# Eleven weight loads issued by ScalarE and not by GpSimd, and running products of 527 columns, in a fused attention, spectral and gating kernel

## The chip, the cores and the metric

The kernel runs on one core of a Trainium2 chip. Its five instruction streams are named as in the profile: PE is TensorE, DVE is VectorE, ACT is ScalarE, POOL is GpSimd and SP is SyncE. SPq, ACTq and POOLq are the instructions by which an engine starts a DMA transfer. The metric is the device time of one execution in microseconds (us); 0.2% of it, about 1.2 us, is what a measurement of this kernel can tell from no change.

## The reference

Three blocks follow each other on tensors of batch 4, sequence 768, width 384 (8 heads of 48). The second and the third get weights as 64-bit floats; the first has none.

```python
# block 1, per head: a decaying state
for t in range(S):
    state = alpha[:, :, t, :, None] * state + np.einsum('bhd,bhe->bhde', k[:, :, t], v[:, :, t])
    y[:, :, t] = np.einsum('bhd,bhde->bhe', q[:, :, t], state)
# block 2
theta = x @ w_theta
y = np.einsum('ts,bsd->btd', w_tok_r, x * np.cos(theta)) + np.einsum('ts,bsd->btd', w_tok_i, x * np.sin(theta))
u = x + y
x = u + np.maximum(u @ w_ch, 0.0)
# block 3
h = np.maximum(x @ w_in, 0.0); u, v = h[..., :512], h[..., 512:]
v_n = (v - v.mean(-1)) / np.sqrt(v.var(-1) + 1e-6)
out = (u * (np.einsum('ts,bsd->btd', w_spatial, v_n) + b_spatial)) @ w_out
```

## The kernel before

Block 1 is cut into 24 units `u` (4 batches, 6 stretches of 128 positions, each with two chunks of 64). A unit loads its decay factors (`load_al`, tile `al`), its queries and keys (`load_qk`) and its values (`load_v`). `att_scan` makes running products of the decay factors: on a line of 8 segments (one for each head of a partition's group) of `SEG` = 67 columns, so 536 in all, it scans backwards (L357), takes one reciprocal for each segment (L360) and scans forwards (L361). `att_qk` (L369) multiplies queries and keys by the result, and small matmuls (`att_a`, `att_k`, `att_u`, `att_y`) make the unit's output, which a pair of DMAs (`move_a`, L401, tile `ay`) feeds with half of its masked scores. Then come a transpose, the theta matmuls (`th_p`), sine and cosine on ACT, and the token mixing (`tokmix`, L610) that gathers a batch in PSUM.

The weights of block 2 come as 64-bit numbers and are made into pairs of 32-bit ones by pieces. A piece `n` passes through five steps. `raw_f64` (L233) starts the load of up to 772 KB into one of two `raw` buffers. `top` (ACT, L239) takes the top 16 bits, `join` (DVE, L248) joins them with the rest, `high` (ACT, L259) rounds and `low` (DVE, L267) takes the remainder; `low` needs `high`. Pieces 0 and 1 are the theta weights, 2 to 13 the token weights, 14 and 15 the channel weights; later ones belong to block 3. The first sixteen are started in the order 13, 1, 2, 0, 3, 7, 4, 8, 5, 15, 6, 9, 14, 10, 11, 12. Since there are two buffers, each load but the first two waits until `join` of the piece two places ahead has read its buffer: piece 2 waits for `join` of 13, piece 14 for `join` of 6.

GpSimd starts these sixteen (`c["queue"] = nc.gpsimd if n < NQ else nc.sync`, NQ = 16) and has little else to do until the third block. SP starts all other loads, save two at the very start that ACT starts. The order of all steps is a hand-kept list of numbers, `ORDER`; each engine runs its steps in that order, and waits for others by semaphores.

Of the kernel before, what the change touches and what calls it, by code (L numbers as in the profile page):

```python
# [35 lines left out]
SEG = 67  # L36
# [30 lines left out]
WM = 1  # L67
NQ = 16
# [64 lines left out]
def attention_mixer_kernel(  # L133
# [45 lines left out]

    p2 = ctx.enter_context(tc.tile_pool(name="p2", bufs=2))  # L180
    wst = ctx.enter_context(tc.tile_pool(name="wst", bufs=2))
# [821 lines left out]
    def load_cst():  # L1003
        nc.scalar.dma_start(cst_sb, cst)
# [435 lines left out]
```

## Time and profile before

| what | value |
|---|---|
| median of 3 runs | 584.64 us (584.15 to 585.07) |
| profiled execution, its own time | 583.91 us |
| its span, first to last instruction | 582.1 us |
| PE busy | 560.0 us (96%) |
| DVE busy | 440.7 us (76%) |
| ACT busy | 252.3 us (43%) |
| POOL busy | 25.1 us (4%) |
| chain that ended last | PE 78%, DVE 10% |

An engine's busy time is an average over stages. What the table does not tell is which engine sets the pace in which stage; that is read from the stretches and from the chain of waits.

### The profile page before, as it was taken

How to read it: one execution, taken by the hardware profiler on the slowest of the kernel's cores; microseconds unless marked ns; L12 is line 12 of the kernel's file. 1: busy time of each engine (PE TensorE's matmuls, PEld its weight loads, DVE VectorE, ACT ScalarE, POOL GpSimd, SP SyncE). 2: the span in 40 equal slices, each digit the busy share in tenths (PEclk: the TensorE clock that was granted, in tenths of full speed). 3: DMA queues.
4: the chain of work that ended last, by engine and by line, in shares of the span. 5: the costliest groups of instructions: out<-in, count | busy, mean ns of one | idle time of the engine just before them, and what ended most of it. 6: DMA issues, size and time to landing. Idle time of an engine off the chain costs nothing.

```text
span 582.1 us, 13446 instructions
## 1 busy us (share of the span) xinstructions
PE 560.0 (96%) x5737; PEld 508.6 (87%) x5737; DVE 440.7 (76%) x769; ACT 252.3 (43%) x474; POOL 25.1 (4%) x45
## 2 busy tenths in 40 slices
PE   2799999999999999999999999999999999999997
PEld 1667878888988889988989899999999899989997
DVE  7999999988788876878755887776665775677470
ACT  3476765535335533334554443534323441343222
POOL 1101100000000000000000100000000100011000
PEclk9999999999999999999999999999999999999999
DMA  7978746454253333333344525001002010211002
GB/s 266 327 240 273 268 158 214 120 191 130 84 171 107 104 91 127 122 106 96 95 133 173 182 81 192 1 0 57 25 2 96 28 42 0 82 42 41 1 1 81
DMA packets 28219, 66.23 MB, mean 114 GB/s; under 512 B 3072, under 2 KB 14336, under 8 KB 27904
## 3 DMA queue, kind: packets, MB, share of 16 engines
q1 hardware_dynamic: 25696, 53.14, 27.4%
q0 software_dynamic: 2176, 11.86, 5.9%
q8 instruction: 45, 0.74, 0.5%
q10 hardware_dynamic: 288, 0.37, 0.2%
q14 instruction: 14, 0.11, 0.1%
HBM read 52.78 MB, written 9.44 MB: 107 GB/s over the span
## 4 chain that ended last, share of the span: by engine, by line
PE 78%; DVE 10%; ACT 1%; DMA 1%; issue 1%; POOL 1%; POOLq 0%; DVEq 0%; ACTq 0%
PE acc L610 22%; PE acc L929 11%; PE pu L861 8%; PE psc L652 7%; PE po L987 6%; PE psv L788 6%; PE sp L900 4%; PE th L534 3%; PE psuy L466 3%; PE th L537 2%; PE psa L383 2%; PE psuy L424 2%; DMA raw<-in_w 1%; PE psk L407 1%; PE pst L494 1%
## 5 line engine op out<-in xcount | busy, mean ns | idle before, releaser
L610 PE MATMUL acc<-w,zs 128*128 128x256 f32 (+1 forms) x828 | 165.9, 344 | 0.0
L610 PEld LDWEIGHTS acc<-w,zs 128*128 128x128 f32 x828 | 128.2, 188 | 15.7
L788 PE MATMUL psv<-w,xs 128*128 128x512 f32 x216 | 53.6, 395 | 0.0
L861 PE MATMUL pu<-xs,w 128*128 128x384 f32 x288 | 53.1, 337 | 0.0
L987 PE MATMUL po<-w,gs 128*128 128x384 f32 x288 | 52.3, 336 | 0.3 <-ACT v L799 0.3
L987 PEld LDWEIGHTS po<-w,gs 128*128 128x128 f32 x288 | 50.2, 188 | 1.6 <-ACT v L799 0.7
L861 PEld LDWEIGHTS pu<-xs,w 128*128 128x128 f32 x288 | 50.4, 188 | 0.7 <-ACT o L997 0.3
L788 PEld LDWEIGHTS psv<-w,xs 128*128 128x128 f32 x216 | 40.0, 187 | 8.2 <-ACT v L799 0.2
L652 PE MATMUL psc<-us,wch 128*128 128x384 f32 (+1 forms) x243 | 41.2, 320 | 0.0
L652 PEld LDWEIGHTS psc<-us,wch 128*128 128x128 f32 x243 | 37.8, 189 | 0.8
L541 ACT ACTIVATE kk<-th,magic 128x384 f32<-128x384 f32 x24 | 13.9, 578 | 53.4 <-PE th L537 53.4
L973 ACT CAST gs<-t 128x384 fp32r<-128x384 f32 x32 | 15.8, 513 | 48.1 <-DVE t L966 48.1
L811 POOL TENSOR_TENSOR rs<-rs,mhalf 128x1 f32<-128x1 f32 x24 | 15.6, 652 | 441.6 <-DVE rs L808 441.6
L357 DVE TENSOR_TENSOR_SCAN al<-al,heads 112x536 f32<-112x536 f32 x24 | 30.5, 1269 | 3.2 <-DMA al<-in_al 3.2
L534 PE MATMUL th<-wth,xh 128*128 128x384 f32 x144 | 31.1, 352 | 1.2 <-DVE r L551 1.0
L361 DVE TENSOR_TENSOR_SCAN al<-al,heads 112x536 f32<-112x536 f32 x24 | 30.6, 1275 | 0.8
L929 PE MATMUL acc<-w,mx 128*128 128x384 f32 x162 | 30.7, 338 | 0.0
L929 PE MATMUL acc<-wt,vns 128*128 128x384 f32 x162 | 30.5, 337 | 0.0
L369 DVE TENSOR_TENSOR qk<-qk,al 112x1024 f32<-112x1024 f32 x24 | 29.3, 1219 | 0.1
L929 PEld LDWEIGHTS acc<-wt,vns 128*128 128x128 f32 x162 | 28.5, 188 | 0.1
L929 PEld LDWEIGHTS acc<-w,mx 128*128 128x128 f32 x162 | 28.5, 188 | 0.1
L239 ACT ACTIVATE zeros<-raw 128x768 f16<-128x768 bf16 (+1 forms) x22 | 22.9, 1043 | 11.6 <-DMA raw<-in_w 11.6
(122 smaller groups left out, 975.7 us busy)
## 6 DMA issues: line engine op xcount, KB each, us to landing
qk<-in_qk SPq DMA_DIRECT2D x24, 512.0 KB, 4.7
raw<-in_w POOLq DMA_DIRECT2D x14, 772.0 KB, 6.1
vd<-in_v SPq DMA_DIRECT2D x24, 288.0 KB, 3.7
al<-in_al SPq DMA_DIRECT2D x23, 268.0 KB, 3.5
raw<-in_w SPq DMA_DIRECT2D x6, 772.0 KB, 5.4
out<-o SPq DMA_DIRECT2D x24, 192.0 KB, 1.9
x2d<-xT SPq DMA_DIRECT2D x6, 576.0 KB, 4.6
ay<-ax SPq DMA_DIRECT2D x48, 64.0 KB, 2.8
```

Of the source, the lines that this page charges most:

```text
L239: nc.scalar.activation(out, c["top"].rearrange("p (c k) -> p c k", k=4)[:, :, 0], AF.Identity, scale=0.5)
L357: nc.vector.tensor_tensor_scan(out=back[:, ::-1], data0=line[:, ::-1], data1=one[:, ::-1], initial=1.0, op0=ALU.mult, op1=ALU.add)
L361: nc.vector.tensor_tensor_scan(out=line, data0=line, data1=one, initial=0.0, op0=ALU.mult, op1=ALU.add)
L369: nc.vector.tensor_tensor(out=x, in0=x, in1=st[u]["ar"], op=ALU.mult)
L534: nc.tensor.matmul(th, xh[:, 0, k], wth[:, pr, k], start=(k == 0 and pr == 0), stop=False)
L610: nc.tensor.matmul(acc[b, n][:, c0:c1], zs[:, pl, ri, m * 128:(m + 1) * 128], w[:, pr, t0:t1], start=first and n != 1, stop=last, skip_gro ...
L652: nc.tensor.matmul(ps, wch[:, pl, k, m * 128:(m + 1) * 128], us[:, pr, k], start=(n == 0), stop=(n == 3 * KD - 1),)
L788: nc.tensor.matmul(ps, xs2[:, pl, k, o:o + 128], win[pr, "v"][:, k], start=(n == 0), stop=(n == 3 * KD - 1),)
L861: nc.tensor.matmul(pu, win[f // 2][:, pl, k * 256 + f % 2 * 128:k * 256 + f % 2 * 128 + 128], xq[b, h][:, pr, k], start=(n == 0), stop=(n ...
L900: nc.tensor.matmul(sp[:, :TH], vns[b, s][:, pl, f * 128:(f + 1) * 128], wsp[s][:, pr, t], start=(n == 0), stop=(n == 3 * NS - 1),)
L929: nc.tensor.matmul(g, left(b, n, j, pl, c), right(n, j, pr), start=(n in (1, 5, 6) and i == 0), stop=(i == 3 * NJ - 1), skip_group_check=n ...
L987: nc.tensor.matmul(po, gs[b][:, pl, f, s * 128:(s + 1) * 128], wo[f // 2][:, pr, f % 2 * DM:(f % 2 + 1) * DM], start=(n == 0), stop=(n == ...
```

## The change

Three edits, of which the first two do something to the running kernel:

- Pieces 2, 0, 3, 7, 4, 8, 5, 15, 6, 9 and 14 (the third to the thirteenth in the order of loading) are started by ACT. Pieces 13, 1, 10, 11 and 12 stay with GpSimd.
- A segment has 66 columns in place of 67. The marks of `heads` move from a segment's first column to its last, the backward scan leaves out the line's first column and the forward scan its last, so each runs over 527 columns in place of 536; a load of decay factors has 264 KB in place of 268.
- The step `warm` gets the number 0 in place of the last number. All numbers in `ORDER` move up by one, and each engine's steps stand in the order in which they stood. New options that are off (ZA, GQ, RS, RP, AH, FIN, SA) come along.

```diff
-SEG = 67
+SEG = 66
+RA = (2, 0, 3, 7, 4, 8, 5, 15, 6, 9, 14)
...
-    nc.vector.memset(heads[:, :, 0:1], 1.0)
+    nc.vector.memset(heads[:, :, SEG - 1:SEG], 1.0)
...
-            c["queue"] = nc.gpsimd if n < NQ else nc.sync
-            k = step(0.0, "queue" if n < NQ else "dma", 2.4 * size, raw_f64, n, after=before, tiles=[raw])
+            c["queue"] = nc.scalar if n in RA else nc.sync if n in RS or n >= NQ else nc.gpsimd
+            k = step(0.0, "act" if n in RA else "dma" if n in RS or n >= NQ else "queue", 2.4 * size, raw_f64, n, after=before, tiles=[raw])
...
+    def scans(u, g0, g1, which):
+        al, rt, one = (x[:, g0:g1].rearrange("p g j -> p (g j)") for x in (st[u]["al"], st[u]["rt"], heads))
+        if "b" in which:
+            nc.vector.tensor_tensor_scan(
+                out=rt[:, :0:-1], data0=al[:, :0:-1], data1=one[:, :0:-1], initial=1.0, op0=ALU.mult, op1=ALU.add
+            )
+        if "i" in which:
...
+                nc.vector.reciprocal(out=out, in_=total)
+        if "f" in which:
+            n = (g1 - g0) * SEG - 1
+            nc.vector.tensor_tensor_scan(out=al[:, :n], data0=al[:, :n], data1=one[:, :n], initial=1.0, op0=ALU.mult, op1=ALU.add)
...
     def att_scan(u):
-        nc.vector.tensor_tensor_scan(
-            out=back[:, ::-1], data0=line[:, ::-1], data1=one[:, ::-1], initial=1.0, op0=ALU.mult, op1=ALU.add
-        )
-        nc.vector.reciprocal(out=al[:, :, 1:2], in_=rt[:, :, 2:3])
-        nc.vector.tensor_tensor_scan(out=line, data0=line, data1=one, initial=0.0, op0=ALU.mult, op1=ALU.add)
+            scans(u, 0, 8, "f" if u in RP else "bif")
...
-    step(0.0, "act", 0.3, warm)
```

On GpSimd, the loads of the kernel before stood in one row from the start of the program (`raw` is the buffer, `in_w64` cut to `in_w` the weights; the pieces of 1552 columns are the half-sized ones, 1 and 15):

```order
L218 MEMSET zeros 128x768
L233 DMA raw<-in_w 128x3088
L233 DMA raw<-in_w 128x1552
L233 DMA raw<-in_w 128x3088 x7
L233 DMA raw<-in_w 128x1552
L233 DMA raw<-in_w 128x3088 x6
L811 ISA
```

Now there are five: pieces 13 and 1 at the start, and 10, 11 and 12.

```order
L230 MEMSET zeros 128x768
L245 DMA raw<-in_w 128x3088
L245 DMA raw<-in_w 128x1552
L245 DMA raw<-in_w 128x3088 x3
L863 ISA
```

On ACT, the start of the program read as follows in the kernel before (L239 is `top`, L259 `high`, L411 copies keys, L482 and L506 copy a unit's output and its transpose, L501 rounds that):

```order
L239 ACTIVATE zeros<-raw 128x768
L411 COPY kt<-acc 128x448
L259 ACTIVATE w<-wf 128x768
L239 ACTIVATE zeros<-raw 128x384
L259 ACTIVATE wth<-wf 128x384
L239 ACTIVATE zeros<-raw 128x768
L411 COPY kt<-acc 128x448
L482 COPY x<-psy 128x4x48 x2
L239 ACTIVATE zeros<-raw 128x768
L506 COPY xT<-pst 128x3x128
L259 ACTIVATE wth<-wf 128x768
L501 CAST xh<-pst 128x384
```

Now the loads of pieces 2, 0, 3 and 7 stand among these, most of them right ahead of the `high` (L271) that waits for the same `join`. In brackets are the semaphores that a row waits for: DVE is the `join` whose buffer is reused, DMAHW the landing of an earlier transfer started by SP or ACT (eight semaphores are shared in turn by all of those).

```order
L454 COPY kt<-acc_125 128x448 [waits PE_49]
L245 DMA raw<-in_w 128x3088 [waits DVE_49]
L271 ACTIVATE w<-wf 128x768
L251 ACTIVATE zeros<-raw 128x384 [waits DMASW1_49]
L245 DMA raw<-in_w 128x3088 [waits DMAHW2_49,DVE_49]
L271 ACTIVATE wth<-wf 128x384
L251 ACTIVATE zeros<-raw 128x768 [waits DMAHW7_49]
L245 DMA raw<-in_w 128x3088 [waits DMAHW5_49,DVE_49]
L454 COPY kt<-acc_224 128x448 [waits PE_49]
L530 COPY x<-psy 128x4x48 [waits PE_49] x2
L251 ACTIVATE zeros<-raw 128x768 [waits DMAHW2_49]
L554 COPY xT<-pst 128x3x128 [waits PE_49]
```

Around the load of piece 14, the last that ACT starts, the rows of ACT were these before:

```order
L580 CAST zs<-z 128x768
L411 COPY kt<-psk 128x448
L259 ACTIVATE w<-wf 128x768
L541 ACTIVATE kk<-th,magic 128x384
L239 ACTIVATE zeros<-raw 128x768
```

Now the load stands between the copy of keys and `high` of piece 6, for whose `join` both wait:

```order
L628 CAST zs<-z 128x768
L454 COPY kt<-psk 128x448
L245 DMA raw<-in_w 128x3088
L271 ACTIVATE w<-wf 128x768
L589 ACTIVATE kk<-th,magic 128x384
L251 ACTIVATE zeros<-raw 128x768
```

## Rows read from the trace of the kernel before

**Rows 1.** Three stretches: bounds and length in us, busy us (instructions) by engine, clock, DMA

```profile
14.50:29.00 14.50, 10.28 (x191) 8.88 (x192) 13.22 (x22) 7.08 (x13) 2.05 (x4) 0.91 0.95 329
36.00:87.00 51.00, 49.51 (x702) 38.98 (x696) 50.08 (x77) 35.70 (x64) 4.65 (x9) 1.00 0.71 240
87.00:500.00 413.00, 412.53 (x4239) 378.27 (x4238) 313.94 (x551) 173.02 (x330) 11.60 (x18) 1.00 0.30 98
```

**Rows 2.** Two pieces of the chain that ended last: start us, us, what

```profile
60.27 7.96 DMA raw<-in_w
...
86.70 1.07 PE acc L610 x6
```

**Rows 3.** DVE in order of time: start us, us, instruction, idle time before it

```profile
10.54 0.93 DVE L248 SCALAR_TENSOR_TENSOR wf<-raw,zeros 128x768 uint32<-128x768 uint32 x1
...
12.38 0.96 DVE L267 SCALAR_TENSOR_TENSOR w<-wf,w 128x768 fp32r<-128x768 f32 x1
...
17.35 0.96 DVE L248 SCALAR_TENSOR_TENSOR wf<-raw,zeros 128x768 uint32<-128x768 uint32 x1 [0.73 <-ACT zeros L239]
...
24.80 0.55 DVE L519 TENSOR_TENSOR xh<-pst,xh 128x384 fp32r<-128x384 f32 x1
...
32.91 0.55 DVE L551 SCALAR_TENSOR_TENSOR r<-kk,th 128x384 f32<-128x384 f32 x1 [0.60 <-ACT kk L541]
...
45.65 0.95 DVE L267 SCALAR_TENSOR_TENSOR w<-wf,w 128x768 fp32r<-128x768 f32 x1
...
61.04 0.95 DVE L267 SCALAR_TENSOR_TENSOR w<-wf,w 128x768 fp32r<-128x768 f32 x1
...
69.38 0.96 DVE L248 SCALAR_TENSOR_TENSOR wf<-raw,zeros 128x768 uint32<-128x768 uint32 x1 [0.65 <-ACT zeros L239]
```

**Rows 4.** POOL starts the loads of pieces 2, 7 and 14

```profile
11.77 0.53 POOL L233 DMA_DIRECT2D raw<-in_w  x1 [9.12 <-DVE wf L248]
...
23.78 0.53 POOL L233 DMA_DIRECT2D raw<-in_w  x1 [4.65 <-DVE tmp L447]
...
60.27 0.53 POOL L233 DMA_DIRECT2D raw<-in_w  x1 [7.19 <-ACT kt L411]
```

**Rows 5.** ACT in order of time, around the same pieces

```profile
11.51 0.84 ACT L259 ACTIVATE w<-wf 128x768 fp32r<-128x768 f32 x1 [0.79 <-DVE wf L248]
...
16.25 1.07 ACT L239 ACTIVATE zeros<-raw 128x768 f16<-128x768 bf16 x1 [1.55 <-DMA raw<-in_w]
...
24.27 0.46 ACT L501 CAST xh<-pst 128x384 fp32r<-128x384 f32 x1
...
31.37 1.08 ACT L239 ACTIVATE zeros<-raw 128x768 f16<-128x768 bf16 x1 [2.46 <-DMA raw<-in_w]
...
44.63 0.84 ACT L259 ACTIVATE w<-wf 128x768 fp32r<-128x768 f32 x1 [0.94 <-DVE wf L248]
...
60.05 0.84 ACT L259 ACTIVATE w<-wf 128x768 fp32r<-128x768 f32 x1
...
68.26 1.09 ACT L239 ACTIVATE zeros<-raw 128x768 f16<-128x768 bf16 x1 [0.63 <-DMA raw<-in_w]
```

**Rows 6.** ACT starts a transfer at the program's start: start us, us

```profile
1.17 0.46 ACTq L342 DMA_DIRECT2D al<-in_al  x1
```

**Rows 7.** SP starts transfers: start us, us, instruction, count

```profile
39.45 1.11 SPq L401 DMA_DIRECT2D ay<-ax  x2
...
91.56 0.33 SPq L233 DMA_DIRECT2D raw<-in_w  x1
...
113.13 1.16 SPq L347 DMA_DIRECT2D qk<-in_qk  x1
```

**Rows 8.** DMA issues of whole pieces: KB each, median us from issue to landing

```profile
raw<-in_w POOLq DMA_DIRECT2D x14, 772.0 KB, 6.1
...
raw<-in_w SPq DMA_DIRECT2D x6, 772.0 KB, 5.4
```

**Rows 9.** DVE to 87 us, scan groups: busy us, mean ns of one | idle before

```profile
L361 DVE TENSOR_TENSOR_SCAN al<-al,heads 112x536 f32<-112x536 f32 x8 | 10.2, 1275 | 0.3
```

More of the change, by code (lines that the diff above doesn't have):

```diff
@@ L67 @@
 WM = 1
+ZA = 0
+AQ = (("load_cst",), ("load_al", 1))
+GQ = ()
+RA = (2, 0, 3, 7, 4, 8, 5, 15, 6, 9, 14)
+RS = ()
+RP = ()
+AH = 0
+FIN = 0
+SA = ()
 NQ = 16
@@ L334, in attention_mixer_kernel, with issuer @@
     tmps = {}
+    def issuer(*key):
+        return nc.scalar if key in AQ else nc.gpsimd if key in GQ else nc.sync
     def load_al(u):
@@ L346, in load_qk @@
         st[u]["qk"] = t[:112]
-        nc.sync.dma_start(t, qk_in[u])
+        issuer("load_qk", u).dma_start(t, qk_in[u])
     def load_v(u):
@@ L351, in load_v, with att_half, att_back, att_inv @@
         st[u]["vd"], st[u]["vn"] = v[:, 0:2], v[:, 2]
-        nc.sync.dma_start(v.rearrange("p c a e -> p (c a e)"), v_in[u])
-    def att_scan(u):
-        al, rt = st[u]["al"], st[u]["rt"]
-        line, back, one = (x.rearrange("p g j -> p (g j)") for x in (al, rt, heads))
-        nc.vector.tensor_tensor_scan(
-            out=back[:, ::-1], data0=line[:, ::-1], data1=one[:, ::-1], initial=1.0, op0=ALU.mult, op1=ALU.add
-        )
-        nc.vector.reciprocal(out=al[:, :, 1:2], in_=rt[:, :, 2:3])
-        nc.vector.tensor_tensor_scan(out=line, data0=line, data1=one, initial=0.0, op0=ALU.mult, op1=ALU.add)
+        issuer("load_v", u).dma_start(v.rearrange("p c a e -> p (c a e)"), v_in[u])
+    def scans(u, g0, g1, which):
[5 more added lines that the diff above has]
+        if "i" in which:
+            out, total = st[u]["al"][:, g0:g1, 0:1], st[u]["rt"][:, g0:g1, 1:2]
+            if u in RP:
+                nc.gpsimd.tensor_tensor(out=out, in0=total, in1=minus_one[:112, None, :].to_broadcast([112, g1 - g0, 1]), op=ALU.pow)
+            else:
+                nc.vector.reciprocal(out=out, in_=total)
+        if "f" in which:
+            n = (g1 - g0) * SEG - 1
+            nc.vector.tensor_tensor_scan(out=al[:, :n], data0=al[:, :n], data1=one[:, :n], initial=1.0, op0=ALU.mult, op1=ALU.add)
+    def att_half(u):
+        scans(u, 0, 4, "bif")
+    def att_back(u):
+        scans(u, 0, 8, "b")
+    def att_inv(u):
+        scans(u, 0, 8, "i")
+    def att_scan(u):
+        if AH and u == 0:
+            scans(u, 4, 8, "bif")
+        else:
+            scans(u, 0, 8, "f" if u in RP else "bif")
     def decay(u, c):
         rt = st[u]["rt"].rearrange("p (a c) j -> p a c j", c=2)
-        return rt[:, :, c, 2:3].to_broadcast([112, NP, D])
+        return rt[:, :, c, 1:2].to_broadcast([112, NP, D])
     def att_qk(u):
@@ L400, in move_a @@
         for par in range(2):
[L401 removed]
+            issuer("move_a", u).dma_start(ay[64 * par:64 * par + 64], ax[64 * (1 - par):64 * (1 - par) + 64])
     def att_k(u):
@@ L433, in att_s @@
         tmp = st[u]["psu", 0][:112] if c and summed(u) else tmps.pop(0)
+        if (u, c) in SA:
+            rt = st[u]["rt"].rearrange("p (a c) j -> p a c j", c=2)
+            for a in range(NP):
+                nc.scalar.activation(ss[:, a], tmp[:, a], AF.Identity, scale=rt[:, a, c, 1:2])
+            return
         nc.vector.tensor_tensor(out=ss, in0=tmp, in1=decay(u, c), op=ALU.mult)
@@ L997, in o_e, with o_l, o_x @@
         nc.scalar.copy(out=o, in_=s2.pop(("po", b, s)))
+    def o_l(b, s, n):
+        if n == 0:
+            s2["o", b, s] = s2["o"].rearrange("p (n e) -> p n e", n=2)[:, take("o", (b, s))]
+        c = slice(n * DM // 2, (n + 1) * DM // 2)
+        (nc.vector.tensor_copy if n else nc.scalar.copy)(out=s2["o", b, s][:, c], in_=s2["po", b, s][:, c])
+    def o_x(b, s, n):
+        c = slice(n * DM // 2, (n + 1) * DM // 2)
+        (nc.sync if n else nc.scalar).dma_start(out[b, s * 128:(s + 1) * 128, c], s2["o", b, s][:, c])
     def o_d(b, s):
@@ L1003, in load_cst @@
     def load_cst():
-        nc.scalar.dma_start(cst_sb, cst)
+        issuer("load_cst").dma_start(cst_sb, cst)
     def warm():
@@ L1012, in negate, with by @@
                 nc.scalar.activation(x, ident, AF.Identity, scale=-1.0)
-    step(0.0, "dma", 0.32, load_cst)
+    def by(*key):
+        return "act" if key in AQ else "queue" if key in GQ else "dma"
+    step(0.0, "act", 1.5, warm)
+    step(0.0, by("load_cst"), 0.32, load_cst)
     if XLP or THP:
@@ L1134, in attention_mixer_kernel @@
             continue
-        step(0.0, "dve", 0.41, acc_zero, b, tiles=[ta[1]])
+        step(0.0, *(("act", 0.5) if ZA else ("dve", 0.41)), acc_zero, b, after=[("load_cst",)] if ZA else [], tiles=[ta[1]])
     for b in range(B):
@@ L1356, in attention_mixer_kernel @@
             t += 2.09
+            if FIN and b == B - 1 and s == NS - 1:
+                e = [step(0.0, x, 0.25, o_l, b, s, n, after=[k], tiles=[ps, o, ("zeros", 1, "o")]) for n, x in enumerate(("act", "dve"))]
+                for n in range(2):
+                    step(0.0, "dma" if n else "act", 0.65, o_x, b, s, n, after=e[n:n + 1], tiles=[o, ("zeros", 1, "o")])
+                continue
             k = step(0.0, "act", 0.375, o_e, b, s, after=[k], tiles=[ps, o, ("zeros", 1, "o")], by=t + 1.0)
```

43 lines of the change are left out of this document (32 added, 11 removed), and 100 rows, old and new, of the table ORDER.

## The prediction

> **What bounds the kernel now.** I read the stretches first [rows 1]. From 87 to 500 us PE is busy 412.53 of 413.00 us: nothing that shortens another engine there moves the end, and whatever moves the point at which PE gets into this stretch moves the end one for one. Between 36 and 87 us it is DVE that has no time left (50.08 of 51.00 us), while PE has 1.5 us of gaps. The chain of waits says the same: it runs along DVE up to 86 us and along PE from 86.70 us [rows 2]. So the change, all of which lies ahead of 87 us save scans, is worth what it does to DVE's order of work there.
>
> DVE loses little to waits, and the reader should see whom it waits for [rows 3]: 0.73 us at 17.35 and 0.65 us at 69.38 for ACT's `top`, which itself waited for a piece to land [rows 5]; 0.60 us at 32.91 for ACT's L541, which stands right behind the `top` of piece 7, and that one had waited 2.46 us for its landing [rows 5]. These three, 1.98 us, hang on late pieces.
>
> **The change, part by part.**
>
> *Scans.* A scan takes 1275 ns for 536 columns [rows 9], 2.4 ns a column with its fixed part spread over all; 9 columns fewer are 9 x 2.4 = 21 ns. Eight units of two scans lie ahead of 87 us, so 16 x 21 = 0.34 us of DVE at most. Some of it, in the first 36 us, only lengthens a wait; I take 0.25 us. The scans behind 87 us lie beside PE's work and are worth nothing. The 1.5% smaller load of decay factors is nothing that a row here could show.
>
> *Loads leave GpSimd.* That frees 11 x 0.53 us of an engine that is idle [rows 4], worth nothing by itself. What counts is when a piece lands. `join` of piece 13 ends at 10.54 + 0.93 = 11.47 [rows 3]; ACT goes on 0.04 us later, at 11.51 [rows 5], GpSimd starts piece 2 only at 11.77 [rows 4]. An ACT that is free starts a load 0.26 us sooner. From issue to landing the medians are 6.1 us for pieces from GpSimd and 5.4 us for the later ones from SP [rows 8], under different loads of the DMA engines, which move 329 GB/s at a busy share of 0.95 between 14.5 and 29 us [rows 1]. With the DMA engines so full the bounds of the difference are 0 and 0.7 us, and a loss of 0.25 us isn't excluded either. I take 0.25 us of gain, nearer to the full stretch.
>
> *Loads enter ACT's row.* ACT started a transfer in 0.46 us [rows 6]; SP took 0.33 us for a single one of these pieces, 0.55 us for each of a pair, and 1.16 us once [rows 7]. I take 0.42 us, between the single piece and the pair, since some of these come just beside SP's. Eleven are 4.6 us of an engine that is busy 35.70 of 51 us [rows 1], and whoever stands behind one in ACT's row waits for it. Most stand right ahead of the `high` for whose `join` both wait, so no new wait for DVE arises, only the 0.42 us. Each load also waits for the landing of a transfer eight such transfers earlier. For piece 6, started after the `high` of 44.63, that is the first of SP's pair at 39.45, over 5 us before [rows 5, 7], and for the others the distance is larger; I put that at nothing.
>
> *Where it comes out on DVE.* I follow it from wait to wait.
>
> 1. Piece 2 goes ahead of `high` at 11.51. DVE's `low` started at 12.38, 0.03 us behind the end of that `high` (12.35) [rows 3, 5]: it slips by 0.42 us, less 0.08 us for four shorter scans, 0.34 us. At 17.35 DVE had 0.73 us to spare. Piece 2 starts 0.26 us sooner and lands 0.25 us sooner, so DVE needs to wait no longer than to 16.84, and it now arrives at 17.35 - 0.73 + 0.34 = 16.96. It is 0.4 us ahead.
> 2. The masked scores of unit 0 came in the delayed part, so their transfer and the unit's output come 0.34 us later, hence ACT's copy, `top` and `join` of piece 0; then piece 7 goes ahead of `high` of piece 0 and L501. DVE's L519 at 24.80 followed ACT's L501 (24.27 + 0.46 = 24.73) at once [rows 3, 5]: 0.34 + 0.42, less a scan or two, is 0.7 us behind.
> 3. At 32.91 DVE had 0.60 us to spare. Piece 7 starts at about 23.9 in place of 23.78 and lands 0.25 us sooner: ACT's `top` of 31.37 comes 0.1 us sooner, so does L541, and DVE with it. What was lost at 24.80 is gone, 0.1 to 0.2 us ahead.
> 4. From there to 69 us DVE has no gap to lose anything in. Where `low` had some slack behind `high`, that is taken off: piece 15's load delays a `high` that ended at 45.47 for a `low` at 45.65 (0.24 us exposed), piece 14's one that ended at 60.89 for a `low` at 61.04 (0.27 us) [rows 3, 5]. With the other loads, which stand behind a `high` or beside longer work, 0.5 us; DVE is then 0.3 us behind.
> 5. At 69.38 the wait of 0.65 us for piece 14 takes that up too. This is the last wait for a piece that ACT starts, so what counts at the end is when piece 14 lands. ACT can start it at 60.23, behind its copy of keys, so 0.04 us sooner than GpSimd at 60.27 [rows 4]; with 0.25 us of quicker landing that is 0.29 us. DVE arrives at 69.38 - 0.65 + 0.3 = 69.03, in time for the `join` at 69.09.
>
> *Sum.* 0.29 us ahead at 69.38, 0.08 us more from the four scans up to 87 us, and 0.1 us given back where PE and ACT need the delayed results: about 0.25 us, which PE carries to the end. The profiled execution would take 583.91 - 0.25 = 583.7 us; it lies 0.73 us below the median of 584.64 us, so as a median I forecast 584.4 us, no change that can be told from none.
>
> A rule speaks against the term of landing. The Trainium skill, DMA: Bandwidth & Descriptors, section "Issuing engines are not separate DMA queues", says that transfers run on the same 16 DMA engines whichever engine starts them, and that a change of issuer saves only sequencer time. By it the 0.25 us fall away and the sum would be 0.0 us.
>
> **The rivals.**
>
> *Faster.* ACT's issues are covered: they begin while ACT still works on what stands ahead of them, and cost what SP's single one cost or less. Then the 1.98 us of late pieces may vanish, with 0.34 us of scans: 2.3 us at most, 1.2 us when half of the waits and all scans go. PE's clock helps: it was granted at 0.91 of full speed from 14.5 to 29 us [rows 1], so some of this stretch ran at the lower of its two levels, 1.2 GHz; if PE is fed more steadily there, up to 0.09 x 14.5 = 1.3 us of it come back, of which DVE could use the 0.60 us at 32.91. Against it: `join` frees the buffer late and ACT waits for that same `join`, so in most places nothing covers the issue. I place it at 583.0 us.
>
> The same side has another mechanism: the descriptors of GpSimd's transfers are held up while DVE works, and ACT's would not be. The trace shows an even 0.53 us for each of the three issues [rows 4], also with DVE busy all the time, so nothing of a hold-up in the issue itself; piece 14 took 7.96 us to land all the same [rows 2]. By this mechanism it would land 1.5 to 2 us sooner, and by step 5 the gain ends where DVE arrives: 0.35 + 0.08 us, 584.2 us, still within the forecast's own range. The Trainium skill, DMA: Bandwidth & Descriptors, section "SWDGE vs HWDGE vs iDMA", states this rule: GpSimd writes descriptors into SBUF, from which DVE locks it out in some modes, and transfers started by ACT are immune.
>
> *Slower.* An issue on ACT, between running activations and beside SP's, takes as long as SP's longest, 0.8 to 1.16 us. Its place is step 4: with 1.0 us an issue the exposed parts are 0.82 us for piece 15, 0.85 us for piece 14 and, as an estimate, about half an issue each for pieces 6 and 9, which stand beside longer work, 2.6 us in all, and the 0.65 us at 69.38 can't take them up: 2.6 - 0.65 = 1.9 us and more, 586.5 to 587 us. It decides from about 0.7 us an issue. For it: ACT is the one engine besides DVE that is in every loop of this stretch. Against it: ACT's own row says 0.46 us.
>
> *It doesn't do what it says.* The order shows the loads on ACT, so this is left out.
>
> **How the numbers follow.** Forecast (within 0.2%, 1.2 us either way): 0.58. Faster by more: 0.26, the covered issue or the steadier clock. Slower by more: 0.16, the long issue. The likeliest time is 584.4 us. The forecast's own bounds: an issue of 0.33 us and 0.7 us of quicker landing give 0.9 us of gain; an issue of 0.6 us and a landing 0.25 us later give 1.1 us of loss: 583.7 to 585.7 us as a median. To reach half-way into both rivals I take 582.9 to 586.0 us.
>
> **What would show it.** In the profile after: ACTq issues of 0.33 to 0.6 us (0.7 us or more: slower); DVE's waits at 17.35 and 32.91 nearly gone, that at 69.38 at most halved, with small new ones behind ACT's `high` and its rounding of transposes (L501 here); the medians of landing from ACT about 0.25 us under those from GpSimd; scans of about 1.25 us; the chain still turning from DVE to PE near 86 us. I am wrong if PE gets into its unbroken stretch more than 1.2 us away from now, or if it no longer stays full afterwards.

## Result and profile after

The changed kernel is slower: 588.28 us median (587.17 to 591.68, 7 runs) against 584.64 us (583.91 to 585.23, 7 runs) for the kernel before; the ratio is 1.0077 with an interval of 1.0058 to 1.0096. Run again it had 587.63 us against 584.64 us, ratio 1.0051 (1.0037 to 1.0065). Forecast was no change, 584.4 us (582.9 to 586.0 us); the time lies outside the range.

The profiled execution took 587.17 us with a span of 585.1 us, 3.26 us more than that of the kernel before. I read it in the order of the prediction. First the three stretches (columns as in [rows 1]):

```profile
14.50:29.00 14.50, 11.04 (x193) 9.57 (x193) 13.12 (x23) 6.91 (x12) 0.00 (x0) 1.00 0.90 329
36.00:87.00 51.00, 48.53 (x710) 38.48 (x699) 49.65 (x77) 35.74 (x63) 1.58 (x3) 1.00 0.72 243
87.00:500.00 413.00, 412.50 (x4230) 377.44 (x4229) 312.40 (x548) 173.31 (x331) 11.61 (x18) 1.00 0.30 97
```

POOL has nothing left to do in the first stretch, and the clock is 1.00 there where it was 0.91 [rows 1]. In the last one PE is as full as before (412.50 of 413.00 us) and got through 4230 matmuls where it got through 4239. That count alone tells little, since it moves with what the ends of the stretch cut off: with 66 columns alone (e7 below), at the pace of before, it is 4230 too. Whether a full engine has become slower has to be read between two fixed moments.

The scans and the landings, as groups (columns as in [rows 8] and [rows 9]):

```profile
raw<-in_w ACTq DMA_DIRECT2D x10, 772.0 KB, 4.8
raw<-in_w SPq DMA_DIRECT2D x6, 772.0 KB, 4.9
raw<-in_w POOLq DMA_DIRECT2D x4, 772.0 KB, 7.1
```

```profile
L389 DVE TENSOR_TENSOR_SCAN al<-al,heads 112x527 f32<-112x527 f32 x8 | 10.0, 1256 | 0.3
L378 DVE TENSOR_TENSOR_SCAN al<-al,heads 112x527 f32<-112x527 f32 x8 | 10.0, 1250 | 3.0 <-DMA al<-in_al 3.0
```

A scan is 19 ns shorter, as forecast (21 ns). Pieces from ACT land in 4.8 us (6.1 us from GpSimd [rows 8]; the four that are left with it, the very first among them, take 7.1 us). But in front of the backward scan (L378) stand 3.0 us of waits for a load of decay factors (1.6 us before, all of it in the first 10 us); 0.8 us of them are in the stretch where DVE has no time left.

DVE in order of time (columns as in [rows 3]); L260, L279, L482 and L495 are L248, L267, L434 and L447 of before:

```profile
11.06 0.93 DVE L260 SCALAR_TENSOR_TENSOR wf<-raw,zeros 128x768 uint32<-128x768 uint32 x1
...
13.28 0.96 DVE L279 SCALAR_TENSOR_TENSOR w<-wf,w 128x768 fp32r<-128x768 f32 x1 [0.72 <-ACT w L271]
...
22.43 0.36 DVE L495 TENSOR_TENSOR tmp<-acc,ss 112x192 f32<-112x192 f32 x1 [1.03 <-PE acc L467]
...
25.98 0.56 DVE L567 TENSOR_TENSOR xh<-pst,xh 128x384 fp32r<-128x384 f32 x1 [0.28 <-ACT xh L549]
...
41.62 1.26 DVE L378 TENSOR_TENSOR_SCAN al<-al,heads 112x527 f32<-112x527 f32 x1 [0.80 <-DMA al<-in_al]
```

The waits at 17.35, 32.91 and 69.38 us [rows 3] are gone, where the forecast had left up to half of the last one. New are 0.72 us behind ACT's `high` at 13.28 us, 1.03 us for PE at 22.43 us and 0.80 us for the decay factors of unit 4.

ACT and its queue (columns as in [rows 5] and [rows 6]), the load of piece 2, the `high` of piece 13, `top` of piece 7, the loads of pieces 8 and 14:

```profile
12.03 0.34 ACTq L245 DMA_DIRECT2D raw<-in_w  x1
12.41 0.84 ACT L271 ACTIVATE w<-wf 128x768 fp32r<-128x768 f32 x1 [1.41 <-DVE wf L260]
...
31.45 1.08 ACT L251 ACTIVATE zeros<-raw 128x768 f16<-128x768 bf16 x1 [1.96 <-DMA raw<-in_w]
...
35.45 0.34 ACTq L245 DMA_DIRECT2D raw<-in_w  x1
...
60.89 0.33 ACTq L245 DMA_DIRECT2D raw<-in_w  x1
```

An issue costs 0.33 to 0.35 us. `high` begins 0.42 us behind the end of `join` (11.06 + 0.93), where it was 0.04 us.

### The profile page after: what moved, and what is told of

Its sections match the earlier page's. It is cut to its first block, busy times and chain, and to the rows that moved or that the text cites. A ratio compares the mean times of both kernels' runs of the same rounds, so it can differ in the third digit from the quotient of the medians.

```text
span 585.1 us, 13439 instructions
## 1 busy us (share of the span) xinstructions
PE 561.8 (96%) x5737; PEld 510.4 (87%) x5737; DVE 439.9 (75%) x769; ACT 252.7 (43%) x474; POOL 19.1 (3%) x34
## 4 chain that ended last, share of the span: by engine, by line
PE 79%; DVE 11%; DMA 4%; ACT 3%; issue 2%; POOL 1%; ACTq 0%; DVEq 0%; POOLq 0%; SPq 0%
PE acc L658 23%; PE acc L981 10%; PE pu L913 7%; PE psc L704 7%; PE po L1039 7%; PE psv L840 6%; PE sp L952 4%; PE th L582 4%; PE psuy L514 3%; DMA raw<-in_w 3%; PE th L585 2%; PE psa L426 2%; PE psuy L467 2%; DVE wf L260 1%; PE psk L450 1%
## 5 line engine op out<-in xcount | busy, mean ns | idle before, releaser
L378 DVE TENSOR_TENSOR_SCAN al<-al,heads 112x527 f32<-112x527 f32 x24 | 30.0, 1250 | 4.6 <-DMA al<-in_al 4.4
L389 DVE TENSOR_TENSOR_SCAN al<-al,heads 112x527 f32<-112x527 f32 x24 | 30.1, 1256 | 0.8
L582 PEld LDWEIGHTS th<-wth,xh 128*128 128x128 f32 x144 | 25.2, 193 | 3.8 <-ACT xh L549 2.5
```

The costliest lines, as they stand in the source:

```text
L378: nc.vector.tensor_tensor_scan(out=rt[:, :0:-1], data0=al[:, :0:-1], data1=one[:, :0:-1], initial=1.0, op0=ALU.mult, op1=ALU.add)
L389: nc.vector.tensor_tensor_scan(out=al[:, :n], data0=al[:, :n], data1=one[:, :n], initial=1.0, op0=ALU.mult, op1=ALU.add)
L582: nc.tensor.matmul(th, xh[:, 0, k], wth[:, pr, k], start=(k == 0 and pr == 0), stop=False)
```

## Where the 3.26 us are

To split the account I take two moments that every kernel has: the start of the last `psk` matmuls (L407 of before) ahead of PE's full stretch, and the start of ACT's last copy of an output. Between them nearly everything is PE, one matmul behind the other. In order of time (start us, us, instruction), of the kernel before:

```profile
86.09 0.51 PE L407 MATMUL psk<-cst_sb,qk 112*128 112x112 f32 x3 [0.54 <-DVE ax L391]
...
578.89 0.48 ACT L997 COPY o<-po 128x384 f32<-128x384 f32 x1 [1.60 <-PE po L987]
```

and of the changed kernel:

```profile
86.64 0.60 PE L450 MATMUL psk<-cst_sb,qk 112*128 112x112 f32 x4 [0.54 <-DVE ax L434]
...
581.51 0.48 ACT L1049 COPY o<-po 128x384 f32<-128x384 f32 x1 [1.63 <-PE po L1039]
```

So PE gets to its full stretch 0.55 us later, needs 494.87 us for it and not 492.80 us (2.07 us more), then come 3.55 us to the span's end (3.24 us before, 0.31 us more) and 2.11 us outside the span (1.78 us, 0.33 us more). 0.55 + 2.07 + 0.31 + 0.33 = 3.26 us. This is the account of one execution of each kernel; the medians are 3.64 us apart.

The largest part lies where the prediction had placed nothing of the change but a few scans of no worth. The diff holds one thing that the section on the change left out and the prediction did not price: a constant that no instruction uses.

```diff
     nc.vector.memset(mhalf, -0.5)
+    minus_one = const.tile([128, 1], F32, name="minus_one")
+    if RP:
+        nc.vector.memset(minus_one, -1.0)
```

RP is empty, so nothing is written; but by the program's layout the constant takes 32 bytes of each partition, and the tiles that are laid out behind it, the weights `w` among them, move up by 32 bytes. Tiles laid out from the other end (`zs`, `gs`) stay. The traces hold no addresses; where this document speaks of them, it goes by the layout.

## Experiments

Each kernel is compared with runs of the kernel before on the same chip. The last columns are from the profiled execution: start of `psk`, and the time from there to the last copy.

| kernel | median us | before us | ratio (interval) | psk us | to last copy us |
|---|---|---|---|---|---|
| before | | | | 86.09 | 492.80 |
| changed | 588.28 | 584.64 | 1.0077 (1.0058-1.0096) | 86.64 | 494.87 |
| e1 changed, again | 587.63 | 584.64 | 1.0051 (1.0037-1.0065) | 87.11 | 494.82 |
| e2 constant alone | 586.34 | 584.64 | 1.0029 (1.0017-1.0040) | 85.48 | 494.50 |
| e3 changed, no constant | 586.56 | 584.64 | 1.0037 (1.0017-1.0057) | 88.71 | 493.21 |
| e4 eleven loads alone | 586.50 | 584.64 | 1.0043 (1.0023-1.0063) | 86.96 | 493.18 |
| e5 without piece 8 | 586.32 | 584.39 | 1.0032 (1.0019-1.0045) | 87.92 | 493.41 |
| e6 piece 8 alone | 585.06 | 584.39 | 1.0013 (0.9998-1.0028) | 87.33 | 492.77 |
| e7 66 columns alone | 583.20 | 584.39 | 0.9980 (0.9968-0.9993) | 85.03 | 492.83 |
| e8 two constants | 585.39 | 584.39 | 1.0007 (0.9995-1.0020) | 87.03 | 493.56 |
| e9 piece 8 later | 586.67 | 584.58 | 1.0048 (1.0019-1.0077) | 88.34 | 493.17 |
| e10 eleven loads, again | 587.55 | 584.58 | 1.0051 (1.0028-1.0074) | 85.99 | 493.31 |
| e11 66 columns, piece 8 on SP | 584.10 | 584.58 | 0.9999 (0.9988-1.0011) | 85.56 | 492.83 |
| e12 constants on both sides | 585.31 | 584.58 | 1.0009 (1.0000-1.0019) | 86.02 | 493.52 |
| e13 first four loads | 585.16 | 584.31 | 1.0015 (1.0001-1.0029) | 88.84 | 493.15 |
| e14 last seven loads | 584.32 | 584.31 | 1.0005 (0.9991-1.0019) | 87.93 | 493.06 |
| e15 without piece 2 | 586.75 | 584.31 | 1.0035 (1.0021-1.0050) | 87.14 | 492.86 |
| e16 six loads behind `high` | 584.48 | 584.31 | 1.0009 (0.9995-1.0024) | 87.99 | 492.91 |
| e17 66 columns, again | 584.11 | 584.12 | 0.9996 (0.9984-1.0009) | 86.44 | 492.84 |
| e18 mended change | 584.94 | 584.12 | 1.0009 (0.9995-1.0024) | 88.60 | 492.84 |

The start of `psk` moves by up to 3.8 us between profiled executions, and by 1.0 and 1.4 us between two executions of one kernel (e4 and e10, e7 and e17), so of that column a single number proves little. The last column repeats within 0.05 us (changed and e1), 0.01 us (e7 and e17) and 0.13 us (e4 and e10).

### Taking the change apart (e1 to e4)

e1 is the changed kernel as it is.

> The changed kernel once more, on the chip of the next three. All theories: 1.005 to 1.010 of the kernel before, as in its first runs (1.0077). If the runs fall again into a group near 587.5 us and one near 591 us, and those near 591 us have a lower mean granted clock, the slower group is PE's clock; if they don't, the first spread was the chip's.

e2, on the kernel before:

```diff
     nc.vector.memset(mhalf, -0.5)
+    minus_one = const.tile([128, 1], F32, name="minus_one")
```

> The kernel before with nothing but one more constant of 4 bytes, never used, which the changed kernel also allocates; it moves the weights, the transposes and most later tiles by 32 bytes. Layout theory (PE's cadence in its full stretch drifts by 0.4% because its operands start at other addresses): +1.5 to +2.5 us, the drift between 87 and 560 us there again, the turn to PE still at 86.7 us. Loads theory (all of the loss comes from ACT's loads and the clock): no change, 584.6 us within 0.5 us.

e3 takes the three lines of the constant out of the changed kernel.

> The changed kernel without the unused constant, so the large tiles lie where they lay before. Layout theory: 1.5 to 2.5 us faster than the changed kernel, about 585.2 us, no drift behind 87 us. Loads theory: as the changed kernel, 587 to 588.5 us.

e4, on the kernel before:

```diff
+RA = (2, 0, 3, 7, 4, 8, 5, 15, 6, 9, 14)
-            c["queue"] = nc.gpsimd if n < NQ else nc.sync
+            c["queue"] = nc.scalar if n in RA else nc.gpsimd if n < NQ else nc.sync
```

> The kernel before with the eleven loads started by ACT alone; 67 columns a segment, no new constant. Layout theory: within 0.8 us of the kernel before (585 us), since only the 0.5 us at the turn to PE is left. Loads theory: +2.5 to +4 us, with or without a second group of runs at a lower clock.

The constant alone costs 0.29%, and its cost lies where theory had it: 494.50 us from `psk` to the last copy, 1.70 us more than before, with `psk` not later. Without it the changed kernel needs 493.21 us there and is still 0.37% slower. The loads alone cost 0.43%, 0.38 us of it between the two moments. 1.70 + 0.38 = 2.08 us, the 2.07 us of the changed kernel. The six executions of e1 lie between 586.91 and 588.05 us, with no group near 591 us; what the spread of the first runs up to 591.68 us was stays open.

### What the constant does (e8, e12)

e8 has a second unused constant, so that the tiles move by 64 bytes:

```diff
     nc.vector.memset(mhalf, -0.5)
+    minus_one = const.tile([128, 1], F32, name="minus_one")
+    minus_two = const.tile([128, 1], F32, name="minus_two")
```

> The kernel before with two unused constants of 4 bytes and not one, so that the weights and the other tiles behind the constants move by 64 bytes and not by 32: their addresses stand to multiples of 64 bytes as before. Theory (alignment to 64 bytes): PE's cadence in the stretch from 87 to 560 us is that of the kernel before (about 174 ns for L987), 584.6 us. Rival (any move, or the mere presence of a constant): 586.3 us, PE 1.5 us later over this stretch as with one constant. Rival (by the distance): 64 bytes cost twice as much, 588 us.

e12 has one on the left, and one at the far end of each pool on the right, so that the left tiles move up by 32 bytes and the right ones down by 32:

```diff
+    minus_one = const.tile([128, 1], F32, name="minus_one")
...
     def open_b():
+        pb.tile([128, 1], F32, name="pad_b")
         pb_stack.close()
...
             gs[b] = mpb[0].tile([128, 2, KF, S], F32R, tag="gs", name="gs", bufs=1)
+            if b == 0:
+                mpb[0].tile([128, 1], F32, name="pad_c")
```

> The kernel before with the unused constant of 4 bytes on the left side and one on the right side of the memory, so that nearly all tiles, those on the left 32 bytes up and those on the right 32 bytes down, stand at a multiple of 64 bytes (before: nearly all 32 bytes off such a multiple). Theory A (the two operands of a matmul want the same place within 64 bytes): PE's lines on w and zs, w and gs have their cadence of before (L610 191.6 ns, L987 173.8 ns start to start), 584.6 us. Theory B (where w itself stands counts): the drift of 1.5 us from 87 to 560 us is there as with the left constant alone, 586.3 us. Theory C (multiples of 64 bytes are good): PE is faster than before, under 584 us.

By its median (1.0007) e8 can't be told from the kernel before; the time between the two moments can. By that none of its three theories held: 493.56 us is 0.76 us more than before, less than half of what 32 bytes cost. e12 has 493.52 us, the same within 0.04 us, though its left tiles stand as in e2 and its right ones stand where no other kernel has them. What e8 and e12 have in common is the distance between left and right tiles, 64 bytes less than before. PE's groups from 87 to 580 us by line and form (busy us, mean ns of one | idle before), before:

```profile
L610 PE MATMUL acc<-w,zs 128*128 128x512 f32 x359 | 132.0, 404 | 0.0
...
L987 PE MATMUL po<-w,gs 128*128 128x384 f32 x288 | 52.3, 336 | 0.3 <-ACT v L799 0.3
```

the changed kernel:

```profile
L658 PE MATMUL acc<-w,zs 128*128 128x512 f32 x360 | 133.0, 405 | 0.0
...
L1039 PE MATMUL po<-w,gs 128*128 128x384 f32 x281 | 52.0, 339 | 0.2 <-ACT v L851 0.2
```

e12:

```profile
L611 PE MATMUL acc<-w,zs 128*128 128x512 f32 x359 | 131.8, 403 | 0.0
...
L991 PE MATMUL po<-w,gs 128*128 128x384 f32 x288 | 53.1, 338 | 0.2 <-ACT v L801 0.2
```

One to three nanoseconds a matmul, in groups of hundreds. Added up from start to start in the trace, over the same matmuls as before: those on `w` and `zs` (717) lost 0.54 us in e2, 0.65 us in e1, and gained 0.19 us in e8 and 0.19 us in e12; those on `w` and `gs` (267) lost 0.79, 0.79, 0.67 and 0.67 us; those on `w` and `mx` (162) gained 0.19, 0.18, 0.19 and 0.20 us. In e4, where no tile moved, all three are within 0.02 us of before. These lines make 1.14 us of the 1.70 us of e2; the rest is spread over others. So the runs fit a pace that goes with the distance between the addresses of a matmul's two operands, and neither the address of `w` alone (e2 against e12) nor the presence of a constant (e2 against e8) fits them. A kernel with both operands moved alike, the direct test, was not run. Theory A (distance) named the quantity that fits, but its rule (same place within 64 bytes is as before) is refuted by `w` and `gs`; which distances are good is open. The Trainium skill, TensorE: Matmul & The Clock Gate, section "Step-by-step: what each phase is for", says that loading the next weights doesn't take read bandwidth from a running matmul. No run here tests that by itself; the 3 ns of L987 show that where the operands lie matters all the same.

### What the columns give (e7, e17)

```diff
-SEG = 67
+SEG = 66
```

with the marks of `heads` and the columns of the scans as in the changed kernel, nothing else.

> The kernel before with 66 columns for each product (527 columns a scan) and nothing else: loads on GpSimd, no further constant. Scans of 1250 ns and not 1270 ns; 16 of them ahead of 87 us. All theories: 584.3 us, 0.0 to 0.5 us below the kernel before. If it is slower by 0.5 us or more, the change of width moves a buffer to a worse place, and that would be part of the loss.

> 66 columns alone once more, on another chip if it so falls. If the columns are what gained 0.2% there: ratio 0.997 to 0.999 again. Rival (the earlier result was luck of the executions; the next kernel with the same columns and one load moved to SP came out at 0.9999): 0.9995 to 1.001.

0.20% faster once, and 0.04%, not told from zero, the other time. The forecast of 0.25 us for the scans (0.04%) lies just outside the first interval and in the midst of the second.

### Which load, which wait (e5, e6, e9, e10, e11)

In the changed kernel ACT starts piece 8 at 35.45 us, and SP the fifth load of decay factors (unit 4) at 35.71 us. The chain of waits (start us, us, what) goes through that load:

```profile
24.33 7.09 DMA raw<-in_w
...
35.71 5.88 DMA al<-in_al
41.62 1.27 DVE al L378
```

In the kernel before SP began it at 35.64 us, GpSimd's piece came 0.25 us behind, it landed in 3.0 us, and DVE's scan didn't wait. Hence the theory that the small transfer (268 KB) is held up by a large one (772 KB) that comes just ahead.

e5 leaves piece 8 out of `RA`, e6 has `RA = (8,)`, both on the kernel before.

> The kernel before with ten of the eleven loads on ScalarE; piece 8 stays on GpSimd. No further constant, 67 columns. Theory (order of transfers): with all eleven, ACT's load of piece 8 begins at 35.45 us, just ahead of SP's fifth load of decay factors (35.8 us), whose landing then takes 5.4 to 6.0 us and no longer 3.0 us, so that DVE's scan of 40.7 us waits some 1 to 2 us. With piece 8 on GpSimd that transfer lands in about 3 us again, the wait in front of that scan is gone, and the time falls from 586.5 us to about 585.2 us. Rival A (the issues themselves cost ACT too much): only one eleventh of the loss goes, 586.3 us, and the scan waits all the same for something else. Rival B (what lies outside the span, 0.3 us, and many small waits): 586 us.

> The kernel before with piece 8 alone started by ScalarE, the other ten by GpSimd. Theory (order of transfers): SP's fifth load of decay factors lands 5.4 to 6 us after its issue and DVE's scan of unit 4 waits 1 to 2 us as with all eleven; 585.7 to 586.5 us. Rival A (the issues cost): 584.8 us, no difference that can be told. Rival B: the landing is late but DVE takes the loss up in later waits (69.38 us): 584.7 us.

e9 moves the step of piece 8 in the order, e10 is e4 again:

```diff
-        for key in (keys[n] for n in ORDER):
+        row = [keys[n] for n in ORDER]
+        row.remove(("raw_f64", 8))
+        row.insert(row.index(("top", 4)) + 1, ("raw_f64", 8))
+        for key in row:
```

> The kernel before with the eleven loads on ScalarE, piece 8's load moved two places down ACT's row, behind the high part of piece 7 and the top of piece 4, so that it begins at about 36.4 us and not at 35.55 us, behind SP's fifth load of decay factors (35.8 us). Theory (order of transfers): that load lands in about 3 us and not in 5.4 to 6.0 us, DVE's scan of unit 4 doesn't wait for it, and the time is 1 us below that of the eleven loads as they were (585.5 us where those take 586.5 us). Rival (the loads cost elsewhere, in the first 30 us): the scan waits no longer and the time is the same, 586.3 us.

> The same kernel as the earlier run with the eleven loads alone (586.5 us there), on the same chip as the other kernels of this call, to see what in its trace repeats. Theory (order of transfers): the fifth load of decay factors takes over 5 us again and DVE's scan of unit 4 waits for it, unless DVE is later than 41.5 us for another reason; PE's single gap of 0.43 us at 425 us is there again. Rival (chance of one execution): one or both are gone. 586.3 us in either case.

e11 is e7 with `RS = (8,)` and piece 8's step moved right behind the load of decay factors.

> 66 columns, no further constant, loads as before but for piece 8, which SP starts right behind its fifth load of decay factors, so that this order is sure in every execution. Theory (order of transfers): executions in which GpSimd's piece 8 comes first and costs 1.5 us (as in the profile of the kernel with two constants) are gone; 583.0 us, 0.2 to 0.3% below the kernel before. Rival (the order matters only where ScalarE starts the piece): as with 66 columns alone, 0.2% below the kernel before. Against both: SP's issue is in the way of its transfer of masked scores at 39.5 us; no better than the kernel before.

The landing itself behaved as the theory says: with piece 8 ahead on ACT it took 6.01 us in e4, 4.73 in e6, 5.55 in e9, 5.07 in e10; with piece 8 behind, 2.91 in e5 and 2.77 in e11. It isn't tied to ACT or to that order alone: in e8, with all pieces on GpSimd and SP 0.25 us ahead, it took 6.56 us and DVE waited (the expectation of e11 has GpSimd's piece first there, but it came second; start us, us, instruction; SP, POOL, DVE):

```profile
35.25 0.33 SPq L344 DMA_DIRECT2D al<-in_al  x1
```

```profile
35.50 0.53 POOL L235 DMA_DIRECT2D raw<-in_w  x1 [6.98 <-DVE ss L436]
```

```profile
41.83 1.27 DVE L359 TENSOR_TENSOR_SCAN al<-al,heads 112x536 f32<-112x536 f32 x1 [1.48 <-DMA al<-in_al]
```

But it isn't the loss of the loads. e5 has neither the late landing nor the wait, and is 0.32% slower; it had expected 585.2 us and took 586.32. e6 lost 0.13%, with an interval that reaches to no change. e9 told nothing of it: its load of piece 8 still began 0.25 us ahead of SP's. The theory accounts for a wait of 0.3 to 2.0 us where DVE arrives in time, not for the time: e18 below has the longest one (2.0 us, for a landing in 7.05 us), and by its median it is not told from no change. e11 was no better than 66 columns alone.

### The place in ACT's row (e13 to e16, e18)

All kernels with early loads on ACT show DVE waiting 1.0 to 2.9 us for PE's `acc` at 22 to 25 us, those with early loads on GpSimd at most 0.24 us there. The theory was that the way there starts with piece 2, whose issue stands ahead of the `high` of piece 13. e13 and e14 split the loads at 25 us, e15 leaves piece 2 with GpSimd; e16 keeps all eleven on ACT and moves those whose next ACT step is a `high` (pieces 2, 0, 7, 8, 15, 14) right behind it:

```diff
+        row = [keys[n] for n in ORDER]
+        for n in RA:
+            i = row.index(("raw_f64", n))
+            j = next(j for j in range(i + 1, len(row)) if steps[row[j]][1] == "act" and row[j][0] != "raw_f64")
+            if row[j][0] == "high":
+                row.insert(j, row.pop(i))
+        for key in row:
```

> The kernel before with only the first four of the eleven loads (pieces 2, 0, 3, 7, issued up to 25 us) on ScalarE. Theory (early path): piece 2's issue of 0.34 us stands ahead of ACT's high part of piece 13 at 11.9 us; DVE's low part, its masked scores and so the second transfer of masked scores follow 0.7 us later, PE's psy and acc come 0.9 us later and DVE waits 1 us or more for acc at 22 us (0.2 us before); executions in which the lower clock of PE comes on top lose 3 us and are about half of all. So most of the loss of the eleven is here: 585.8 to 586.5 us. Rival (late path: the order of transfers at 36 us, piece 14 and the rest): 584.7 us.

> The kernel before with only the last seven (pieces 4, 8, 5, 15, 6, 9, 14, issued from 28 us) on ScalarE. Theory (early path): 584.8 us, 0.0 to 0.3 us slower; no wait of DVE for acc at 22 us; the spread of the executions is that of the kernel before. Rival (late path): DVE's scan of unit 4 waits 1 to 2 us for the fifth load of decay factors; 585.6 to 586.2 us.

> The kernel before with ten of the eleven on ScalarE, piece 2, the first one, on GpSimd as before. Theory (piece 2's issue ahead of the high part of piece 13 is what makes PE late at 20 us): second transfer of masked scores issued at 14.3 us and not at 15.0 us, no wait over 0.5 us for acc at 22 us, 585.0 us. Rival (any of the early four does it, or the number of loads): 586.3 us.

> The kernel before with all eleven on ScalarE, where those whose next ACT operation is a high part (pieces 2, 0, 7, 8, 15, 14) stand right behind that operation and not ahead of it, so that the issue runs while ACT works. Theory (early path): the high part of piece 13 begins at 11.6 us and not 0.4 us later, PE's psy is back where it was, and the time is 585.0 us, with what remains of the fixed costs (0.3 us outside the span, 0.26 us in PE's one gap at 425 us). Rival (not the place but the queue costs): 586.3 us as with the eleven ahead.

ACT's start in e4 (start us, us, instruction):

```profile
11.90 0.34 ACTq L234 DMA_DIRECT2D raw<-in_w  x1
12.28 0.84 ACT L260 ACTIVATE w<-wf 128x768 fp32r<-128x768 f32 x1 [1.51 <-DVE wf L249]
```

and in e16:

```profile
11.56 0.84 ACT L260 ACTIVATE w<-wf 128x768 fp32r<-128x768 f32 x1 [0.66 <-DVE wf L249]
11.56 0.33 ACTq L234 DMA_DIRECT2D raw<-in_w  x1
```

Behind `high` the issue runs beside it: it delays no instruction of ACT there, and the load starts 0.34 us sooner than in e4. e16 is at 1.0009, not told from no change, where the same eleven loads ahead gave 1.0043 and 1.0051. e18, the changed kernel without the constant and with this order, is at 1.0009 as well.

> The changed kernel without its unused constant and with six of its eleven ScalarE loads right behind the next high part (as in the run with them behind): 66 columns, left tiles where they were, ScalarE's loads out of the way of DVE. If the three parts of the loss are rightly told apart, it is 584.0 us, within 0.1% of the kernel before or up to 0.2% below, while the changed kernel is 0.8% above. Rival (place in ACT's row isn't the cause, the earlier run was luck): 586 us, 0.3% above.

So, by the medians, the loads cost their time where the issues stand ahead, and not because ACT starts them. It isn't one issue: without piece 2 the loss stays (1.0035), the first four alone cost 0.15%, the last seven nothing that can be told. And the trace of e16 doesn't settle which wait went: its profiled execution took 1.80 us more than its median (586.28 us against 584.48 us), and it still waits 1.5 us at 22 us, and 2.3 us at 34 us behind piece 7.

That the issues cost their time by way of PE's lateness at 22 us is not shown, and e15, e16 and e18 speak against the way by piece 2. There the second transfer of masked scores starts at 14.32, 14.35 and 14.55 us, about when it did before (14.31 us), and PE's `psy`, which waits for it, is late all the same, at 20.15, 19.94 and 20.67 us against 19.21 us. What these three share with the other eight kernels that wait is an order: ACT starts the load of piece 0 ahead of that transfer, by 0.07 to 0.14 us, where GpSimd starts it 0.12 to 0.13 us behind. Here are that transfer, the load of piece 0 and `psy`, before:

```profile
14.31 0.58 SPq L401 DMA_DIRECT2D ay<-ax  x1
```

```profile
14.44 0.53 POOL L233 DMA_DIRECT2D raw<-in_w  x1 [2.14 <-DVE wf L248]
```

```profile
19.21 0.35 PE L466 MATMUL psy<-vd,ay 64*64 64x48 f32 x3 [1.00 <-DMA ay<-ax]
```

and in e16:

```profile
14.35 0.73 SPq L402 DMA_DIRECT2D ay<-ax  x1
```

```profile
14.29 0.34 ACTq L234 DMA_DIRECT2D raw<-in_w  x1
```

```profile
19.94 0.35 PE L467 MATMUL psy<-vd,ay 64*64 64x48 f32 x3 [1.69 <-DMA ay<-ax]
```

No kernel changes this order alone, so it is a rival that stands untested. It isn't the whole of it: in the changed kernel, with the same order, `psy` came 4.81 us behind the transfer's start (15.21 to 20.02 us), as before (4.90 us).

Part of what e16 saves isn't a wait behind ACT at all. By the medians its loss is 1.7 and 2.8 us smaller than those of e4 and e10. Of this 0.3 us lie outside the span (1.80 us against 2.11 us) and 0.3 to 0.4 us in PE's full stretch (492.91 us against 493.18 and 493.31 us). The rest, 1.1 to 2.1 us as an estimate from these numbers, must lie ahead of it, and no trace shows where.

e18 doesn't beat the kernel before; of all kernels here only 66 columns alone may, by what the two runs above say.

## Why the prediction was wrong

*What bounds the kernel.* That PE is full from 87 us on was right; that the change, save scans of no worth, therefore lies ahead of 87 us was the step that failed. It took "full" for "at a fixed pace". The constant, a part of the diff that the prediction's list left out as no work, moved one operand of the matmuls by 32 bytes and cost 1.70 us (e2), half of the loss. The sentence on what would prove me wrong (PE late by more than 1.2 us, or no longer full) didn't hold this case either: PE was late by 0.55 us and full.

*Scans.* 19 ns and not 21 ns each; right.

*Landing.* 0 to 0.7 us sooner was the bound, 0.25 us the choice; the median came 1.3 us sooner (4.8 us against 6.1 us), though in later runs of such kernels it was 4.8 to 6.1 us, so that of the medians little is sure. Piece 14 is clear: it landed in 4.34 us where it had taken 7.96 us [rows 2], and in 4.29 to 4.51 us in every kernel that had it on ACT, and 6.3 to 8.4 us in those that hadn't. The rival of held-up descriptors had the right sign there and too small a size (1.5 to 2 us). But with the issuer an order changed: in every kernel that has piece 14 on ACT it starts 0.25 to 0.27 us ahead of SP's load of decay factors and 0.64 to 0.65 us ahead of the load of queries and keys, in every other one 0.25 us behind the first and 0.13 to 0.14 us ahead of the second. So the issuer isn't shown to be the cause. The Trainium skill, DMA: Bandwidth & Descriptors, section "Issuing engines are not separate DMA queues", says that starting transfers on several engines saves only the sequencer's time; for that reason piece 14 neither bears this out nor refutes it. The quicker landing is worth nothing in the end, as step 5 said: the gain ends where DVE arrives.

*Issues.* 0.33 to 0.35 us each, under the 0.42 us taken. The rival of long issues (0.8 us and more) is refuted, though its sign was right. What failed is where they were weighed. Step 1 had the slip of `low` right in kind: 13.28 us against 12.38 us, of which 0.52 us came with a later first `join` (11.06 us against 10.54 us) and 0.38 us from the issue (forecast 0.42 us). Step 2 had it go on into SP's transfer of masked scores, rightly (14.60 us against 13.71 us), but not from there back to DVE by way of PE's `acc`, where it came as a wait of 1.03 us at 22.43 us (0.24 us before). So where step 2 has 0.7 us at 24.80 us, it was 1.18 us (25.98 us). The slip is not the only way to this wait: e15 and e16 have it without the slip.

*The reset at 32.91 us* (step 3) came: `top` of piece 7 began at 31.45 us, 0.08 us later than before [rows 5] and not 0.1 us sooner.

*Steps 4 and 5.* The exposures of 0.5 us were looked for behind `high` and `low`; what came was 0.80 us for decay factors at 41.62 us, a transfer whose landing was in no term. The wait at 69.38 us is gone, where step 5 left 0.06 us of it, and took part of the loss up; 0.55 us were left at 86.64 us.

*Outside.* 0.31 us behind the last copy and 0.33 us outside the span were in no term. Neither comes with the constant or the columns. Behind the last copy, kernels in which a piece has changed its queue (e11 with its one on SP too) have 3.5 to 3.7 us, only e14 has 3.31 us; all others have 3.24 to 3.26 us. Outside the span the changed kernel, e1, e3, e4, e10 and e15 have 2.1 us, all others 1.8 us. The cause of both is open.

*Chances.* Slower had 0.16. Its mechanism was to be the length of the issue; by the runs it was the issues' place, in a way that is open, and the place of the weights in memory. Of the rival on the fast side the clock came true (1.00 where it was 0.91, with PE busy 11.04 us in place of 10.28 us from 14.5 to 29 us), but PE got to its full stretch no sooner. Even the loads alone (586.50 us) lie beyond the range's upper end of 586.0 us.

## What to carry to other kernels

Read the allocation as a part of the diff: a tile that nobody uses moves its neighbours, and a full engine's pace can depend on where its operands lie; compare the time between two fixed moments of the full stretch, not only its busy share. Put a DMA issue on a working engine right behind an operation that already runs, not ahead of one that somebody waits for: the same eleven issues cost 0.4 to 0.5% in the one place and nothing that can be told with six of them in the other. But look at the order in which transfers start as well: it changes with such a move, and a small transfer can land late behind a large one. And when a step slips, follow everything that it feeds, transfers too, up to the next wait that takes it up.

## What the runs showed of the hardware

- PE's pace depends on where the two operands of a matmul lie: 3 ns on 336 ns (L987) when one of them moves by 32 bytes, 1.70 us in 493 us. That it goes by the distance between them fits: two kernels with the same distance and other addresses agree within 0.04 us.
- An issue placed ahead of an ACT instruction delayed it by 0.38 us; placed behind it, it ran at the same time (both at 11.56 us).
- A load of 268 KB that is started within 0.3 us of one of 772 KB on another queue landed in 2.7 to 3.0 us or in 4.5 to 7.1 us; the later times came with the large one ahead, and once (e8) with it 0.25 us behind.
- In the kernels with eleven loads on ACT in the order of the change (and in e5, e9 and e13) DVE pauses at 424 us, between two instructions of its own and with no other releaser, and PE's weights wait for the result (start us, us, instruction; first DVE, then the weight load, of the changed kernel):

```profile
423.66 0.56 DVE L1010 TENSOR_TENSOR t<-acc,bsb 128x384 f32<-128x384 f32 x1 [1.55 <-PE acc L981]
424.67 0.56 DVE L1018 TENSOR_TENSOR t<-t,small 128x384 f32<-128x384 f32 x1 [0.46 <-DVE t L1010]
```

```profile
426.89 0.83 PEld L981 LDWEIGHTS acc<-wt,vns 128*128 128x128 f32 x5 [0.42 <-DVE small L1001]
```

  Between the two moments the kernels that pause and have no further constant need 0.35 to 0.61 us more than the kernel before, those with loads on ACT and no pause (e14, e15, e16, e18) 0.04 to 0.26 us; so the pause goes with most of the 0.38 us of e4. The kernel before doesn't pause at these instructions; why the others do, no run tells.
- In e5 the clock of PE fell to its lower level, 1.2 GHz, from 29.4 to 36 us, after a stretch in which PE was busy 5.19 of 6.50 us, and stayed there while PE was busy all the time (columns as in [rows 1]):

```profile
22.90:29.40 6.50, 5.19 (x125) 3.98 (x121) 4.76 (x9) 4.54 (x8) 0.00 (x0) 0.98 0.69 252
29.40:36.00 6.60, 6.60 (x80) 5.53 (x80) 6.30 (x10) 3.01 (x7) 0.00 (x0) 0.50 0.68 239
```
